# Pre-norm attention and GEGLU block on one core: permutation matmuls in the prologue, the last 512 queries in four chunks of 128, Tanh for the GELU of four chunks

## The chip, the cores and the metric

The kernel runs on one NeuronCore of a Trainium2 chip. Time is device microseconds of one execution; times of before are of three runs. The profile is of one further execution, taken by the hardware profiler.

## The reference, cut to what matters

One sequence of 2048 rows, 640 features, 32 heads of 20; a feed-forward of 1728. All inputs are bf16.

```python
def _A_ref(x, wqkv, wo):                       # H = 32, Dh = 20
    qkv = (x @ wqkv).reshape(B, S, 3, H, Dh).transpose(2, 0, 3, 1, 4)
    q, k, v = qkv[0], qkv[1], qkv[2]
    p = softmax(einsum("bhqd,bhkd->bhqk", q, k) * Dh ** -0.5)
    o = einsum("bhqk,bhkd->bhqd", p, v)
    return o.transpose(0, 2, 1, 3).reshape(B, S, D) @ wo
def _B_ref(x, w_gate, w_up, w_down):
    h = gelu_tanh(x @ w_gate) * (x @ w_up)
    return h @ w_down
h = x + _A_ref(layernorm(x), A_wqkv, A_wo)
out = h + _B_ref(layernorm(h), B_w_gate, B_w_up, B_w_down)
```

## The kernel before, in words

**A planner writes the order.** Every instruction (or small group) is an `op` with an engine, a duration guessed by `c_mm`, `c_act`, `c_dve`, a priority, what it reads and writes, and the PSUM banks it takes and gives back. `Sched.schedule` plays the program through with these durations and picks, for each engine, the ready op of the best priority; `emit` writes the resulting order as a fixed stream for each engine, with semaphore waits. So an engine is a strict queue at run time: an instruction that waits holds all behind it. `P_QK` is the best priority (scores and exponentials), `P_BG` the last (feed-forward). `QK_LEAD` and `PE_AGE` shape when TensorE leaves other work for the next scores; `WARM_*` and `PAD_*` put idle matmuls in to keep its clock up.

**Prologue.** SP loads x in four pieces of 512 rows, then the weights. For each 128 rows `ln_stats` (DVE) or `act_stats` (ScalarE, a Copy and a Square pass with accumulators; rows 512 to 1023) gives mean and variance, `ln_rsqrt` the factor through a Sqrt on ScalarE, `ln_apply` the normalised rows on DVE; five transposes on TensorE and a copy (ScalarE, or DVE for `T_DVE`) give `xnT`. `proj_k`, `proj_q`, `proj_v` project. A group is four heads, each on 32 partitions (20 used, row 0 an offset), so q and k rows must be spread from 20 to 32: `proj_k(0)` and `proj_q(0, 0)` do it by DMAs from the projected tile straight into `kt_all` and `qt_all`, the other groups by way of DRAM. `q_bound0` adds an upper bound of the scores, which needs the largest |k| of all 2048 keys. Idle rows are filled by memsets: two fills of `qt_all` on ScalarE, the others on POOL (`cst`).

**Attention.** `SIZES` cuts the queries into chunks: 512, five of 256, two of 128; a slot is a chunk and `512 / size` groups, 32 slots in all. A tile is 512 score columns of one head; 64 tiles to a slot. `unit` takes three or two tiles in turn (PSUM banks 0-2 and 3-4, `PAT`): score matmuls (L1001), one Exp on ScalarE over 1536 or 1024 columns into `pts` or `rege`, later the products with v (`pv_op`) into bank 6. `D_QUADS` gives the sets of four tiles in each slot whose exponential DVE computes instead (`d_exp`, L925 and some integer and fp16 passes over 1024, or 2048 from slot `D_WIDE` on); for slots in `DA_SLOTS` the last sum of that is an accumulating DMA issued by POOL. `D_LEAD` starts these tiles ahead of their slot. At the end of a slot `epilogue` copies bank 6, transposes it by fp32 matmuls and divides (L1098 to L1107).

**Feed-forward.** When a chunk has all its groups, `post` transposes, projects by `wo`, adds x, normalises, and issues gate matmuls (L1179) and copies (L1214), GELU on ScalarE over up to 2048 columns, up matmuls and products (L1228), then `down` (L1259, L1263). All but the last chunk do this as background while the next chunks' attention runs. Each session of GELU loads its function table and afterwards that of Exp again; `MERGE = (1,)` lets chunks 1 and 2 share one. The last chunk (`tail`) runs alone at the end, with GELU straight from PSUM (L1201, L1204).

Of the kernel before, what the change touches and what calls it, by code (L numbers as in the profile page):

```python
# [7 lines left out]
ALU = mybir.AluOpType  # L8
# [10 lines left out]
WARM_WIN, WARM_MIN = 3.4, 0.5  # L19
PAD_WIN, PAD_MIN = 3.4, 0.42  # L20
QK_LEAD = .65
PE_AGE = 1.5
SD_ALONE = .21
P_SD = 1
# [23 lines left out]
class Sched:  # L48
# [48 lines left out]
    def schedule(self):  # L97
# [23 lines left out]
        while done < total:  # L121
            assert events, "no operation can start"
# [3 lines left out]
            for e in ENGINES:  # L126
# [122 lines left out]
                for o in ([o, join] if join is not None else [o]):  # L249
                    o.start = t0 if o is chosen else free[e]  # L250
                    if e == "act":
                        due = t + o.dur + (0.905 if o.dur > 1.2 else 1.332) - QK_LEAD if o.mode == "exp" else None
# [27 lines left out]
    def emit(self, es, block_of):  # L280
# [3 lines left out]
        prog = {e: [] for e in ENGINES}  # L284
        for o in self.order:
# [8 lines left out]
            for d in o.deps:  # L294
# [78 lines left out]
D_LEAD = ((0,) * 8, (0, 10, 20) + (36,) * 21)  # L373
D_WIDE = 18
RSQRT_MAGIC = float(0x5F3759DF)

P_EV = 1.8
P_QK, P_PV, P_PRO, P_EPI, P_LN, P_BG = 0, 1, 1.5, 2, 2.5, 3
P_LND, P_LNP = 1.9, 2.5


def bass_sequential_preLN__mha_block__glu_gated_geglu__prompt_kernel(
# [12 lines left out]
    with ExitStack() as es:  # L395
# [13 lines left out]
        def c_act(n):  # L409
            return 0.052 + n * 0.000833  # L410
# [8 lines left out]
        off0 = sb("off0", [128, 1], FP32)  # L419
        stats = sb("stats", [128, 4, 2, 6], FP32)  # L420
# [3 lines left out]
        asum = sb("asum", [128, 2, 4], FP32)  # L424
# [34 lines left out]
        carve = carver(regw, W_WORDS)  # L459
        xnT = carve(NA * S).rearrange("p (a s) -> p a s", a=NA)  # L460
        wqk = carve(NA * 1280).rearrange("p (a d) -> p a d", a=NA)
        wv = carve(NA * D).rearrange("p (a d) -> p a d", a=NA)
        k_un = [carve(S), rege[:, 0:S]]
# [10 lines left out]
        xn_p = carve(4 * D).rearrange("p (i d) -> p i d", i=4)  # L474
# [50 lines left out]
        def cst(fn, key, n=128):  # L525
            op(POOL, fn, 0.1 + n * 0.001, P_BG, writes=[key, "pool"])
# [5 lines left out]
        op("act", I("activation", f32(qt_all[:, 1, :, :]), zer[:, 0:2].bitcast(FP32).to_broadcast([128, 2048]), ACT.Copy), 1.8, P_QK,  # L532
           reads=["zer"], writes=["qf1"])
        op("act", I("activation", f32(qt_all[:, 2, :, :]), zer[:, 0:2].bitcast(FP32).to_broadcast([128, 2048]), ACT.Copy), 1.8, P_QK,
           reads=["zer"], writes=["qf2"])
        op("act", I("activation", v_all[:, :, :, DH], zer[:, 0:1].unsqueeze(2).to_broadcast([128, NT, H]), ACT.Copy, bias=1.0), 0.5, P_QK,
           reads=["zer"], writes=["vones"])
        op("dve", I("memset", f32(kt_all[:, 1:4, :]), ones2), 4.2, P_QK, writes=["kf0"])
        cst(I("memset", kt_all[:, 0, :].bitcast(FP32), ones2), "ktm0", 1024)
# [3 lines left out]
        for g in range(4, NG):  # L543
            cst(I("memset", kt_all[:, g, :].bitcast(FP32), ones2), "kf%d" % g, 800)
        cst(I("memset", qt_all[:, 0, 0, :].bitcast(FP32), 0.0), "qtm0", 256)
# [7 lines left out]
        cst(I("memset", sel0, 0.0), "sel0")  # L553
        cst(I("memset", off0[:], 0.0), "off0", 1)
        for j in range(4):
            cst(I("memset", off0[32 * j:32 * j + 1, :], OFF), "off0", 1)
        cst(I("memset", identf[:], 0.0), "identf")
        cst(I("affine_select", out=identf[:], in_=identf[:], compare_op=ALU.not_equal, fill=1.0,
              base=0, pattern=[[-1, 128]], channel_multiplier=1), "identf")
        for g in range(0, NG, 2):  # L560
            cst(I("memset", f32(qt_all[:, 3, g:g + 2, :]), 0.0), "qf3%d" % g, 512)
# [4 lines left out]
        def load(dst, src, key, mb, after=(), writes=None):  # L566
            return op("sp", I("dma_start", dst, src), 0.08, P_BG, writes=writes or [key], after=after,
                      sem=key, lat=mb)
# [7 lines left out]
        load(wqk, A_wqkv[:, 0:1280].rearrange("(a p) d -> p a d", p=128), "wqk", 14.0)  # L576
# [4 lines left out]
        q_fills = [["qf0%d" % g for g in range(1, NG, 2)], ["qf1"], ["qf2"], ["qf3%d" % g for g in range(0, NG, 2)]]  # L581

        e_ops, sqrts = [], []
        T_DVE = (11, 13, 15)
# [11 lines left out]
        def ln_rsqrt(t0, n, prio, table=False, sqrt=False):  # L596
# [7 lines left out]
            d = v if table or sqrt else lambda fn, r, w: op(POOL, fn, 0.25, prio, reads=r, writes=w)  # L604
            d(I("tensor_copy", mv16[:, t0:t0 + n, :], mv[:, t0:t0 + n, :]), [("mv", t) for t in ts], [k16])
            d(I("tensor_scalar", sd16[:, t0:t0 + n], mv16[:, t0:t0 + n, 1], LN_EPS, None, ALU.add), [k16], [ks])
# [5 lines left out]
            if sqrt:  # L612
                sqrts.append(op("act", I("activation", sd16[:, t0:t0 + n], sd16[:, t0:t0 + n], ACT.Sqrt), 0.2, 1, reads=[ks], writes=[ks]))
                v(I("reciprocal", y, sd16[:, t0:t0 + n]), [ks], rk)
                return
            if table:
                op("act", I("activation", sd16[:, t0:t0 + n], sd16[:, t0:t0 + n], ACT.Sqrt), 0.2, -1, mode="sqrt", reads=[ks],
                   writes=[ks])
                v(I("reciprocal", y, sd16[:, t0:t0 + n]), [ks], rk)
                return  # L620
# [10 lines left out]
        def ln_apply(eng, src, dst, dkey, t, rkeys, prio, first=False):  # L631
# [5 lines left out]
            return op(eng, fn, 0.82 if eng == "act" else c_dve(D, 0.46), prio,  # L637
# [18 lines left out]
        def dma_transposes(src, rkeys, dst, wkey, after=()):  # L656
            op("sp", I("dma_start_transpose", dst, src), 1.25, P_EPI, reads=rkeys, writes=[wkey], sem=f"xp{wkey[1]}", lat=2.8, after=after)
# [10 lines left out]
        def act_stats(t0, n):  # L668
            for t in range(t0, t0 + n):
                for f, k in ((ACT.Copy, 0), (ACT.Square, 1)):  # L670
                    op("act", I("activation", junk, x_sb[:, t, :], f, accum_out=asum[:, k, t - t0:t - t0 + 1]), 0.86, 1.4,
                       reads=[f"x{t // 4}"], writes=["junk", ("as", t)])
            m = mv[:, t0:t0 + n, 0]
            rk = [("as", t) for t in range(t0, t0 + n)]
            d = lambda fn, r, w: op("dve", fn, 0.17, P_EPI, reads=r, writes=w)
            d(I("tensor_scalar", m, asum[:, 0, 0:n], 1.0 / D, None, ALU.mult), rk, ["am"])
            d(I("tensor_tensor", asum[:, 0, 0:n], m, m, ALU.mult), ["am"], rk)
            d(I("scalar_tensor_tensor", out=mv[:, t0:t0 + n, 1], in0=asum[:, 1, 0:n], scalar=1.0 / D, in1=asum[:, 0, 0:n],
                op0=ALU.mult, op1=ALU.subtract), rk + ["am"], [("mv", t) for t in range(t0, t0 + n)])

        for t0 in (0, 4, 8, 12):
            if t0 == 4:
                act_stats(4, 4)
            else:
                for t in range(t0, t0 + 4):
                    ln_stats(x_sb[:, t, :], t, [f"x{t // 4}"], 1.4 if t0 == 12 else P_BG)
            ln_rsqrt(t0, 4, P_PRO, sqrt=True)
            for t in range(t0, t0 + 4):
                e_ops.append(ln_apply("dve", x_sb[:, t, :], xn_p[:, t % 4, :], ("xnp", t % 4), t, [f"x{t // 4}"], P_PRO,
                                      first=True))  # L690
                transposes(xn_p[:, t % 4, :], [("xnp", t % 4)], xnT[:, :, t * 128:(t + 1) * 128], ("xnT", t),
# [3 lines left out]

        w_readers = []
# [25 lines left out]
        def proj_qk(col, t, c, dst, dkey, banks, prio, evac, after=(), peak=None):  # L722
            bk = Bank(*banks)
            key = ("bk", sc_id())
            w_readers.extend(chain(bk, key, 512, [(wqk[:, a, col + 128 * t:col + 128 * t + 128],
                                                   xnT[:, a, c * 512:(c + 1) * 512]) for a in range(NA)],
                                   [("xnT", tt) for tt in range(4 * c, 4 * c + 4)] + ["wqk"], prio))
# [18 lines left out]
        def proj_k(t, banks, prio, evac="dve"):  # L746
            for c in range(4):
                src = k_un[t % 2][:, 512 * c:512 * c + 512]
                proj_qk(D, t, c, src, ("ku", t % 2, c), banks, prio, evac, after=e_ops if t == 1 else (), peak=True)
                if t == 0:  # L750
# [24 lines left out]
        def proj_q(t, c, banks, prio, evac="dve"):  # L775
            proj_qk(0, t, c, q_un[:, t, :], ("qu", t), banks, prio, evac)
            if t == 0 and c == 0:
                for j in range(4):
                    q_keys[0][0].append(("q", 0, 0, j))
                    dma(qt_all[32 * j + 1:32 * j + 21, 0, 0, :], q_un[DH * j:DH * j + DH, 0, :], ("q", 0, 0, j),  # L780
                        [("qu", 0), "qtm0"], "qc", 2.2, prio - 0.1)
# [26 lines left out]
        def q_bound0(banks, prio):  # L808
            bk = Bank(*banks)
            key = ("bk", sc_id())  # L810
            w_readers.append(op("pe", lambda eng: eng.matmul(
                bank(bk), sel0.rearrange("p j e -> p (j e)"), aq[0], start=True, stop=True),
                c_mm(512), prio, mode="full", util=0.213, reads=[("aq", 0), "sel0"], writes=[key], acq=[bk]))
            dst = qt_all[:, 0, 0, :]
            q_first.append(op("dve", lambda eng: eng.scalar_tensor_tensor(
                out=dst, in0=bank(bk), scalar=off0[:, 0:1], in1=dst, op0=ALU.add, op1=ALU.add), c_dve(512) + 0.05, prio,
                reads=[key, "off0"] + q_keys[0][0], writes=[("qo", 0, 0)], rel=[bk]))
# [20 lines left out]
        for c, (q0, nq) in enumerate(CHUNKS):  # L838
# [516 lines left out]
```

## Time and profile before

| | |
|---|---|
| median of the runs | 910.08 us (909.8 to 910.76) |
| profiled execution | span 906.4 us; the profile gives no time around it |
| first exponential starts, last one ends | 32.86 us, 875.99 us |
| exponentials on ScalarE | 358 of 1536 columns, 349 of 1024 |
| tiles on DVE | 276 of 2048 |
| activation table loads | 16 |
| granted TensorE clock | 1.000 |

Times of the profile count from the span's start. A group's mean is the time of one instruction by itself; neighbours on an engine overlap a little, so the distance between two starts is shorter than the mean.

### The profile page before, as it was taken

To read this page: it belongs to the slowest core of one execution; us is meant where nothing else is said; L and a number is where in the kernel's file an instruction comes from. 1 tells how busy PE (TensorE), PEld (TensorE's weight loads), DVE (VectorE), ACT (ScalarE), POOL (GpSimd) and SP (SyncE) were. 2 spreads that over 40 slices of the span, in tenths; PEclk is the share of its full clock that TensorE was granted. 3 is DMA by queue.
4 is the path that set the end of the run, shared out by engine and by line. 5 is a ranking of instruction groups with operands and counts; after the bars stand their busy time and mean duration, and the time that the engine had idled before them with its cause. 6 is when DMAs were issued, how large, how long until landed. Compare 5 with 4: busy or idle time off the path is not lost.

```text
span 906.4 us, 25256 instructions
## 1 busy us (share of the span) xinstructions
PE 832.6 (92%) x11167; PEld 376.8 (42%) x11167; DVE 740.7 (82%) x1405; ACT 877.0 (97%) x793; POOL 123.5 (14%) x238
## 2 busy tenths in 40 slices
PE   3999999999898988999999999999999998998998
PEld 2432322222233332334344445444444444656666
DVE  8858898989899997898898877787977996778643
ACT  7899999999999999999999999999999999999992
POOL 5001110000013111111222000030101000101000
PEclk9999999999999999999999999999999999999999
DMA  7213341442634322243263221441432332242110
GB/s 261 84 32 80 69 97 31 106 105 62 198 136 77 56 52 48 48 69 73 49 115 63 48 44 29 84 85 41 93 63 43 75 69 39 58 85 56 33 41 16
DMA packets 52357, 65.97 MB, mean 73 GB/s; under 512 B 20876, under 2 KB 38376, under 8 KB 52248
## 3 DMA queue, kind: packets, MB, share of 16 engines
q0 software_dynamic: 12816, 31.46, 19.4%
q1 hardware_dynamic: 39432, 32.89, 13.2%
q8 instruction: 88, 1.44, 0.7%
q14 instruction: 21, 0.17, 0.1%
HBM read 20.12 MB, written 8.09 MB: 31 GB/s over the span
## 4 chain that ended last, share of the span: by engine, by line
ACT 82%; PE 13%; DVE 4%; POOL 1%; issue 0%
ACT pts L403 52%; ACT rege L403 28%; PE ps L702 4%; PE ps L1001 3%; PE ps L1179 2%; PE ps L403 2%; ACT L403 1%; PE ps L1259 1%; DVE dwx L403 1%; DVE qt_all L925 0%; PE ps L644 0%; DVE rege L1228 0%; ACT qt_all L403 0%; POOL nw L403 0%; DVE rege L925 0%
## 5 line engine op out<-in xcount | busy, mean ns | idle before, releaser
L403 ACT ACTIVATE pts<-ps 128x1536 bf16<-128x1536 f32 (+1 forms) x474 | 565.3, 1373 | 3.9 <-PE ps L403 2.9
L1001 PE MATMUL ps<-qt_all,kt_all 32*128 32x256 bf16 (+2 forms) x4096 | 308.9, 272 | 39.1 <-ACT pts L403 18.1
L403 ACT ACTIVATE rege<-ps 128x1536 bf16<-128x1536 f32 (+1 forms) x233 | 292.7, 1379 | 0.5 <-PE ps L403 0.4
L1001 PEld LDWEIGHTS ps<-qt_all,kt_all 32*128 32x128 bf16 x4096 | 102.4, 92 | 252.8 <-ACT pts L403 128.6
L1179 PE MATMUL ps<-rege,regw 128*128 128x256 bf16 (+2 forms) x1120 | 159.2, 274 | 10.2 <-ACT rege L403 2.7
L403 PE MATMUL ps<-pts,v_all 128*21 128x256 bf16 (+2 forms) x2370 | 124.8, 274 | 0.0
L1179 PEld LDWEIGHTS ps<-rege,regw 128*128 128x128 bf16 x1120 | 86.1, 98 | 62.5 <-issue 27.6
L925 DVE TENSOR_SCALAR rege<-ps 128x512 int16<-128x512 f32 x120 | 81.9, 686 | 22.2 <-PE ps L1001 21.1
L925 DVE TENSOR_SCALAR qt_all<-ps 128x512 int16<-128x512 f32 x104 | 71.2, 686 | 27.1 <-PE ps L1001 26.4
L403 PE MATMUL ps<-rege,v_all 128*21 128x256 bf16 (+2 forms) x1366 | 91.1, 278 | 0.1
L702 PE MATMUL ps<-regw 128*128 128x512 bf16 (+1 forms) x360 | 87.5, 353 | 1.9 <-ACT regw L650 1.5
L1259 PE MATMUL ps<-regw,rege 128*128 128x320 bf16 x448 | 83.8, 302 | 2.5 <-DVE qt_all L925 0.7
L403 DVE TENSOR_TENSOR qt_all<-qt_all 128x1024 int16<-128x1024 f16 (+3 forms) x77 | 68.7, 893 | 1.1
L403 PEld LDWEIGHTS ps<-pts,v_all 128*21 128x21 bf16 x2370 | 54.8, 91 | 32.7 <-issue 27.8
L403 DVE TENSOR_SCALAR qt_all<-qt_all 128x1024 int16<-128x1024 int16 (+3 forms) x106 | 57.9, 549 | 1.6 <-DMA qt_all<-dwx 0.4
L403 DVE TENSOR_TENSOR rege<-rege 128x1024 f16<-128x1024 f16 (+1 forms) x74 | 50.4, 681 | 0.7
L1259 PEld LDWEIGHTS ps<-regw,rege 128*128 128x128 bf16 x448 | 36.4, 98 | 35.0 <-issue 16.6
L403 PE MATMUL ps<-kt_all,zer 128*32 128x512 bf16 x568 | 48.3, 385 | 0.0
L403 DVE TENSOR_SCALAR rege<-rege 128x1024 int16<-128x1024 int16 (+2 forms) x113 | 47.8, 437 | 0.4
L702 PEld LDWEIGHTS ps<-regw 128*128 128x128 bf16 x360 | 28.9, 99 | 44.1 <-issue 24.4
L1214 DVE CAST rege<-ps 128x512 bf16<-128x512 f32 (+1 forms) x53 | 35.9, 678 | 13.3 <-PE ps L1179 13.1
L1228 DVE TENSOR_TENSOR rege<-rege,ps 128x512 bf16<-128x512 bf16 (+1 forms) x53 | 35.7, 676 | 12.2 <-PE ps L1179 12.1
(114 smaller groups left out, 766.2 us busy)
## 6 DMA issues: line engine op xcount, KB each, us to landing
qt_all<-qt_all POOLq DMA_DIRECT2D x9, 512.0 KB, 5.0
qt_all<-dwx POOLq DMA_DIRECT2D x9, 512.0 KB, 4.6
rege<-rege POOLq DMA_DIRECT2D x16, 256.0 KB, 3.5
rege<-dwx POOLq DMA_DIRECT2D x7, 512.0 KB, 4.8
rege<-in_A_x_dram SPq DMA_DIRECT2D x5, 640.0 KB, 5.7
dvx<-qt_all POOLq DMA_DIRECT2D x6, 512.0 KB, 4.8
q_rows<-regw SPq DMA_DIRECT2D x20, 128.0 KB, 2.8
out_dram<-rege SPq DMA_DIRECT2D x16, 160.0 KB, 3.2
```

Source lines behind the costliest of these rows:

```text
L403: return lambda eng: getattr(eng, method)(*args, **kwargs)
L702: yield op("pe", lambda eng, l=l, r=r, k=k: eng.matmul(bank(bk, n), l, r, start=(k == 0), stop=(k == len(steps) - 1)), c_mm(n) + cold, pri ...
L925: d_ops.append(op("dve", lambda eng: eng.tensor_scalar(v[:, 512 * h:512 * h + 512], bank(b), EXP_MUL, -32000.0, ALU.mult, ALU.max), c_dve( ...
L1001: return lambda eng: eng.matmul(out()[:, kk * nq:(kk + 1) * nq], kt_all[32 * j:32 * j + 32, g, kt * 128:(kt + 1) * 128], qt_all[32 * j:32 ...
L1179: op("pe", lambda eng, a=a, f=f, fi=fi: eng.matmul(bank(bk)[:, fi * nq:(fi + 1) * nq], w[:, a, F0[f]:F0[f] + 128], hnT[:, a, 128 * tb:128 ...
L1214: cp.append(op("dve", lambda eng, bg=bg, fv=fv, w=w: eng.tensor_copy(fv, bank(bg, w)), c_dve(w), p, reads=[kg], writes=hkeys(k), rel=[bg], ...
L1228: hdone.append(op("dve", lambda eng, bu=bu, fv=fv, w=w: eng.tensor_tensor(fv, fv, bank(bu, w), ALU.mult), c_dve(w), p, reads=[ku] + hkeys( ...
L1259: op("pe", lambda eng, f=f, o=o, hf=hf, bk=bk: eng.matmul(bank(bk, 320), ha_f[:, o:o + 128], wd[:, f, hf * 320:(hf + 1) * 320], start=(f = ...
```

## The change

It changes several parts at once.

- **Prologue.** A constant `perm` spreads 20 rows to 32 by a matmul: the keys 1536 to 2047 of group 0, and group 0's queries inside `q_bound0`. `wqk` is loaded as `wk` and `wq`; the projections of these keys run in pieces of 128 rows. Statistics on ScalarE go to the last one, one, three, one tiles of each four (`LN1_ACT`), seven of sixteen `ln_apply` to POOL (`LN1_POOL`), small norm steps to POOL, and the fills of `qt_all` and most of `kt_all` to POOL behind the norm.
- **Slots.** The first 512 queries run as one chunk for groups 0 to 5 and as two of 256 for groups 6 and 7; the last 512 in four chunks of 128 (`SIZES`, `QR`). The very last slot is cut into three groups and one. `FOUR`: two slots take two tiles by two. 33 slots. `SIX` (six banks in four slots) goes.
- **DVE's tiles.** 280 instead of 276; fewer slots in `DA_SLOTS`.
- **GELU.** Chunks 4, 6, 7, 8 (`TANH`) form it with Tanh on ScalarE over 512 columns and fp16 steps on DVE, in rounds of 4 (or 2) blocks; the others stay with GELU, chunks 0 and 1 and 2 and 3 in one session each.
- **Tail.** The last chunk's transposes are cut in two, its copies go to DVE, and it has priority `P_END`.
- **Loads and planner.** `w_gate` is loaded from slot 4 on, the feed-forward weights in pieces each behind the one before; constants of the planner change.

```diff
-WARM_WIN, WARM_MIN = 3.4, 0.5
-PAD_WIN, PAD_MIN = 3.4, 0.42
-QK_LEAD = .65
-PE_AGE = 1.5
+WARM_WIN, WARM_MIN = 3.4, 0.53
+PAD_WIN, PAD_MIN = 3.4, 0.46
+QK_LEAD = 0.55
+PE_AGE = 0.5
...
-SIZES = (512, 256, 256, 256, 256, 256, 128, 128)
-BASE = (0, 0, 2, 0, 2, 0, 2, 3)
-SIX = tuple(range(8, 12))
+SIZES = (256,) * 6 + (128,) * 4
+BASE = (0, 2) * 3 + ((0, 2, 3) if len(SIZES) == 9 else (0, 1, 2, 3))
+SIX = ()
+FOUR = (28, 29)
+PERM_C = 3
+FIRST = 6
+QR = ((0, 512),) + CHUNKS
...
-D_LAG = 8
-MERGE = (1,)
+D_LAG = 4
+MERGE = (0, 2)
+TANH = (4, 6, 7, 8)
...
-DA_SLOTS = (1, 2, 3, 5) + tuple(range(9, 32))
+DA_SLOTS = (1, 10, 11, 12, 14, 15, 16, 17, 18, 19, 20, 22, 23, 24, 27, 28, 31)
-D_QUADS = (1,) + (2,) * 11 + (3, 2) * 3 + (2, 2, 3) * 3 + (2,) * 5
+D_QUADS = (0, 2, 2, 2, 2, 2, 2, 1, 2, 2, 2, 2, 3, 2, 3, 2, 3, 2, 3, 2, 3, 2, 3, 2, 3, 2, 3, 2, 3, 2, 2, 2, 0)
+T_DVE = (0, 1, 3, 5, 9, 11, 12, 13, 14)
+LN1_ACT = (1, 1, 3, 1)
+LN1_POOL = (0, 1, 3, 5, 6, 13, 14)
...
-            return 0.052 + n * 0.000833
+            return 0.063 + n * 0.000833
...
-        op("act", I("activation", f32(qt_all[:, 1, :, :]), zer[:, 0:2].bitcast(FP32).to_broadcast([128, 2048]), ACT.Copy), 1.8, P_QK,
-           reads=["zer"], writes=["qf1"])
...
+        for k in range(1, 4):
+            for g in range(0, NG, 2):
+                cst(I("memset", f32(qt_all[:, k, g:g + 2, :]), 0.0), "qf%d%d" % (k, g), 512, e_ops)
...
+        def pieces(dst, src, key, after, m=1):
+            for k in range(0, dst.shape[1], m):
+                n = min(m, dst.shape[1] - k)
+                after = (load(dst[:, k:k + n, :], src[:, k:k + n, :], (key, k), W_LAT, after=after),) + tuple(after)[:0]
...
-                e_ops.append(ln_apply("dve", x_sb[:, t, :], xn_p[:, t % 4, :], ("xnp", t % 4), t, [f"x{t // 4}"], P_PRO,
+                e_ops.append(ln_apply(POOL if t in LN1_POOL else "dve", x_sb[:, t, :], xn_p[:, t % 8, :], ("xnp", t % 8), t, [f"x{t // 4}"], P_PRO,
...
+                if t == 0 and c >= PERM_C:
+                    w_readers.append(op("pe", lambda eng, bp=bp, src=src: eng.matmul(bank(bp), perm[:], src, start=True, stop=True), c_mm(512), prio,
+                                        mode="full", util=0.213, reads=[("ku", 0, c), "perm"], writes=[kp], acq=[bp]))
...
         def q_bound0(banks, prio):
+            w_readers.append(op("pe", lambda eng: eng.matmul(bank(bk), perm[:], q_un[:, 0, :], start=True, stop=False),
+                                c_mm(512), prio, mode="full", util=0.213, reads=[("qu", 0), "perm"], writes=[key], acq=[bk]))
...
-            slots += [(c, tuple(range(g, g + n))) for g in range(0, NG, n)]
+            slots += [(c, tuple(range(g, g + n))) for g in (range(FIRST) if c == 0 else range(FIRST if q0 < 512 else 0, NG, n))]
+        slots[-1:] = [(slots[-1][0], slots[-1][1][:-1]), (slots[-1][0], slots[-1][1][-1:])]
...
-        PAT = [((0, 1, 2), (3, 4, 5)) if s_ in SIX else ((0, 1, 2), (3, 4)) for s_ in range(len(slots))]
+        PAT = [((0, 1, 2), (3, 4, 5)) if s_ in SIX else ((0, 1), (2, 3)) if s_ in FOUR else ((0, 1, 2), (3, 4)) for s_ in range(len(slots))]
...
+            elif c in TANH:
+                for k0 in range(0, nb, nt_):
+                    for k in range(k0, min(k0 + nt_, nb)):
+                        bg, kg = mms(k, wg, "wg", tuple(x for key in hkeys(k) for x in sc.rd.get(key, ())))
+                        op("dve", lambda eng, bg=bg, fv=fv, w=w: eng.tensor_scalar(fv, bank(bg, w), 0.5, None, ALU.mult), c_dve(w), p, reads=[kg],
+                           writes=hkeys(k), rel=[bg], after=first)
+                        d(I("tensor_tensor", z, f2, f2, ALU.mult), 0.53, hkeys(k), [tk], aft)
+                        d(I("tensor_scalar", z, z, 8 * 0.044715 * GELU_C, 2 * GELU_C, ALU.mult, ALU.add), 0.265, [tk], [tk])
+                        d(I("tensor_tensor", z, z, f2, ALU.mult), 0.53, hkeys(k) + [tk], [tk])
+                        tanhs.append(op("act", I("activation", z, z, ACT.Tanh), c_act(w) + 0.04, P_TANH, mode="exp", reads=[tk], writes=[tk]))
+                    for k in range(k0, min(k0 + nt_, nb)):
+                        bu, ku = mms(k, wu, "wu", (sc.lw[tk],))
+                        op("dve", lambda eng, bu=bu, z=z, w=w: eng.scalar_tensor_tensor(
+                            out=z, in0=z.bitcast(F16), scalar=1.0, in1=wide(bank(bu, w)), op0=ALU.add, op1=ALU.mult), c_dve(w), p,
+                           reads=[ku, tk], writes=[tk], rel=[bu])
+                        hdone.append(op("dve", I("tensor_tensor", wide(fv), wide(fv), z, ALU.mult), 0.066 + 0.53 * w / 1024, p,
+                                        reads=[tk] + hkeys(k), writes=hkeys(k)))
...
+                if g == W_EARLY:
+                    pieces(wg, B_w_gate.rearrange("(a p) f -> p a f", p=128), "wg", tuple(w_readers))
```

More of the change, by code (lines that the diff above doesn't have):

```diff
@@ L121, in schedule @@
         while done < total:
+            if not events and due is not None and due > t:
+                events.append(due)
             assert events, "no operation can start"
@@ L293, in emit @@
             need = {}
-            for d in o.deps:
+            deps = set(o.deps)
+            if o.eng == "pool" and o.sem is None:
+                deps.update(pool)
+                pool = [o.i]
+            for d in deps:
                 q = ops[d]
@@ L616, in ln_rsqrt @@
             if table:
[L617 removed]
+                op("act", root, 0.2, -1, mode="sqrt", reads=[k16, "eps"],
                    writes=[ks])
@@ L673, in act_stats @@
             m = mv[:, t0:t0 + n, 0]
+            s0, s1 = asum[:, 0, t0:t0 + n], asum[:, 1, t0:t0 + n]
             rk = [("as", t) for t in range(t0, t0 + n)]
[L675 to L679, printed above, removed]
```

338 lines of the change are left out of this document (208 added, 130 removed).

## Prediction, before the changed kernel was run

> **What bounds the kernel now.** I read the page first (shares of the engines, chain that ended last), then ScalarE's groups kept apart by shape, its timeline, the windows, and the chain in order of time at both ends. The page:
>
> ```profile
> PE 832.6 (92%) x11167; PEld 376.8 (42%) x11167; DVE 740.7 (82%) x1405; ACT 877.0 (97%) x793; POOL 123.5 (14%) x238
> ...
> ACT 82%; PE 13%; DVE 4%; POOL 1%; issue 0%
> ```
>
> ScalarE (ACT) is busy 97% of the span and holds 82% of the chain. Its groups by shape say with what:
>
> ```profile
> L403 ACT ACTIVATE pts<-ps 128x1536 bf16<-128x1536 f32 x238 | 373.3, 1583 | 3.9 <-PE ps L403 2.9 <-PE ps L1001 0.8
> L403 ACT ACTIVATE pts<-ps 128x1024 bf16<-128x1024 f32 x236 | 270.4, 1161 | 0.0
> L403 ACT ACT_TABLE_LOAD x16 | 20.5, 1283 | 1.1 <-PEq L1340 0.8
> ```
>
> Exponentials over 1536 and 1024 score columns alternate, with no idle time before them; 16 table loads cost 1.28 us each. The means overlap, so the price of one is the distance of starts, from the timeline of ACT:
>
> ```profile
> 510.03 4.64 ACT L403 ACTIVATE pts<-ps 128x1536 bf16<-128x1536 f32 x4
> 514.49 2.43 ACT L403 ACTIVATE rege<-ps 128x1536 bf16<-128x1536 f32 x2
> ...
> 539.54 1.28 ACT L403 ACT_TABLE_LOAD   x1
> 540.83 6.46 ACT L403 ACTIVATE rege<-rege 128x2048 bf16<-128x2048 bf16 x4
> 547.31 1.28 ACT L403 ACT_TABLE_LOAD   x1
> ```
>
> The four at 510.03 are two pairs of 1536 + 1024 and take 4.46 us, 2.23 a pair; the two means differ by 0.42. So 1.33 us and 0.905 us. A GELU session is two loads round 3.24 us for each 2048 + 1536 columns (6.48 for two). Windows, in two answers (busy PE, PEld, DVE, ACT, POOL):
>
> ```profile
> 33.00:876.00 843.00, 788.84 (x10700) 345.86 (x10699) 701.10 (x1295) 838.46 (x731) 110.63 (x202) 1.00 0.33 70
> 250.00:300.00 50.00, 43.67 (x649) 16.93 (x646) 47.40 (x103) 49.80 (x43) 12.56 (x33) 1.00 0.38 96
> ```
>
> From the first exponential (32.86) to the end of the last (875.99) ACT hardly rests. And where VectorE (DVE) is 95% busy, 250 to 300, ACT still is at 49.80 of 50: a loaded DVE has not held it up so far. The ends, from the chain in order of time:
>
> ```profile
> 15.86 1.20 ACT regw L650 x2
> ...
> 17.12 4.75 PE ps L702 x14
> ...
> 32.86 4.62 ACT pts L403 x4
> ...
> 874.65 1.34 ACT rege L403
> ...
> 878.82 1.71 ACT rege L403
> ...
> 886.72 3.28 PE ps L1259 x23
> ...
> 891.07 8.01 PE ps L1179 x140
> ```
>
> The prologue waits for ACT until 17.1 and then for PE; after the last exponential come 30.4 us in which a GELU, a projection, a norm and a whole feed-forward of 128 rows go one after the other.
>
> So time = first exponential + ACT's work and stalls to the last one + tail. Before: 32.9 + 843.1 + 30.4 = 906.4, the profiled span. The profile gives no time around the span; the median of the runs is 910.08, so I carry 3.7 us over.
>
> **The middle.** Counted in the built order: before 358 x 1.33 + 349 x 0.905 = 792.0; seven GELU pairs (columns of chunks 0 to 5) x 3.24 = 22.7; ten loads x 1.30 = 13.0. Sum 827.7, so 15.4 of the 843.1 are stalls, mostly pieces of 0.03 to 0.6 us after a 1024.
> After: 332 x 1.33 + 386 x 0.905 = 790.9 (four tiles more go to DVE, but two slots run with 1024 alone); five GELU pairs 16.2, for chunks 4, 6, 7, 8 leave GELU; six loads, since MERGE pairs 0 with 1 and 2 with 3 and only chunk 5 is alone: 7.8; and 19 Tanh of 8960 columns: x 0.000833 = 7.5, and 0.13 for each (3.24 less 3584 x 0.000833, halved) = 2.4, so 9.9. Sum 824.8, 2.9 less. This includes the last chunk but one, whose GELU stood in the tail before.
>
> The loads are priced by their row, 1.28 us. [...]
>
> Stalls: I keep 15.4, and 2 for 19 Tanh that each wait in ACT's queue for DVE, with all exponentials behind them (nothing to 0.5 us each, the size of the stalls of now; 0.1 taken, as the four GELU at 540.83 started right behind their load). New QK_LEAD, PE_AGE and planner costs only reorder PE; they may take half of the stalls away or add as much: 8 either way. Middle: 842.2.
>
> **What covers it.** DVE pays. Added: three 16-bit passes and a last product for each 512 Tanh columns (0.33 + 0.20 + 0.33 + 0.33 us), 17.5 blocks: 21 us. Tiles whose last sum is done by a DMA fall from 240 to 168, so 76 more sums of about 0.30 us (0.61 for two): 22. Four exp tiles more, 1.5 each: 6. One product instead of two in the epilogues: -2. So 47; by distances of starts (0.61 us for a read of 512 from PSUM) the whole of DVE's program, counted line by line, grows from 696 to 744 us. From slot 20 on I count 278 us of DVE against some 300 of ACT, 93%; the same slots had 76%, and single slots of before 93 to 95% (144 to 167, 243 to 269, 635 to 659) without a stall of note. So I charge nothing, and keep the cost of that cover being gone as a rival. POOL issues fewer DMAs; PE's columns are the same: QK for a unit takes 0.33 us as 3 of 512, 6 of 256 or 12 of 128. The pieces of wg, wu and wd stand in SP's queue each behind the landing of the one before; what waits behind them there are x rows and transposes for chunks from 3 on, needed tens of us later.
>
> **The prologue.** Two fills of ACT (3.6 us) move to POOL behind the norm; statistics on ACT grow from 4 tiles to 6 (0.83 a pass), but only two tiles stand ahead of the first root instead of four. DVE does three tiles of x0 to about 8.0 (before: fourth one and others to 11.6); cast on POOL 0.34, root 0.2, reciprocal 0.2: 9.3. Then POOL applies three of the four. The trace has no such POOL row: at least 0.36 (DVE's distance for it), at most 0.07 + 640 x 1.75 ns = 1.2 by the slope of the affine selects (288 ns for 128 columns, 344 for 160). I take 1.1, POOL's own kind: 12.6. Transposes and copy 0.8: first K projection at 13.4 instead of 17.1. PE's list from there to the first scores is as long as before (45 wide matmuls and 20 of 128 against 53), 15.4: first exponential at 28.8. DVE's own list, 20 us of work from 5.2 on, ends earlier, at 27 with the waits. Permutation matmuls replace eight small DMAs of 0.7 us issue; those of K are needed 48 tiles later, those of q before the sum on PE: nothing on the path. Bounds 26.5 (POOL at 0.4) to 32.5.
>
> **The tail.** From the last exponential: PV 0.5; copy of 128 columns instead of 512, one transpose instead of four, reciprocal and product, last transpose and copy, two last Wo steps: 2.9. Two additions and statistics 1.6, one down addition, aggregate and casts 0.7: 5.2; root, reciprocal, apply 0.8: 6.0. PE has 27 down matmuls in its queue ahead of the transposes, 27 x 0.142 from 2.9 on: 6.7; transposes and copy 0.9: feed-forward at 7.6 instead of 15.1 after the end. What follows is unchanged (15.3): 22.9 instead of 30.4. Gone are the switch to GELU and its 1.7, 70 feed-forward matmuls and half the down projection of the chunk before. Bounds 21 to 26.
>
> Sum: 28.8 + 842.2 + 22.9 = 893.9, and 3.7: 897.6 us.
>
> **Rivals.** (a) DVE becomes the bound: 278 us of work in the last third, in a strict order with waits for PE in it. If that order fills DVE to 85% only (the slots of before lie between 66 and 95%), the stretch takes 327 instead of 300, and PE and ACT wait behind late evacuations: 924.6, slower. It decides against the whole gain from 88% down. For it: average 76% before. Against it: the 250-to-300 window. Half of it, 90%, gives 907. (b) POOL's applies come late and the prologue gains nothing: 32.9, so 901.7. For it the rows
>
> ```profile
> L403 POOL TENSOR_SCALAR nw<-nw 128x2 f32<-128x2 f32 x14 | 5.0, 360 | 1.1
> L403 POOL TENSOR_SCALAR nw<-nw 128x1 f32<-128x1 f32 x2 | 0.4, 190 | 0.2
> ```
>
> where one more column, beside a busy DVE, costs 170 ns. [...] (c) Stalls halve under the new lead times (-8), with prologue and tail at their short ends (-2.3, -1.9): 885.4. (d) The change does not do what it says: the built order has ten loads and no load near a Tanh, so I give that nothing.
>
> **How the numbers follow.** Forecast 0.55 (its own range 892 to 904), (b) 0.12, (c) 0.13, (a) in full 0.12, half of it 0.08. A measurement of this kernel tells 0.2%, 1.8 us, from no change: 908.3 to 911.9. Faster: forecast, (b), (c) and half of half-(a): 0.83; same 0.05; slower 0.12. The range reaches from (c) past half of (a) to the last case that is not slower, and leaves out full (a): 885 to 911.
>
> **What would show it.** First exponential near 29 us; ten table loads; exponentials 332 and 386 at unchanged distances; tail near 23 us. Wrong if ACT has idle time before exponentials or Tanh released by DVE or by PE after 550 us, if DVE stands at 99% there, or if POOL's 640-column applies take well over 1.2 us.

## The result, and the profile after

The changed kernel takes 898.12 us (median of four runs, 897.33 to 898.97) against 909.98 (909.8 to 910.76) of the kernel before beside it: ratio 0.987, 95% interval 0.9856 to 0.9884. The forecast was 897.6. The profiled execution has a span of 895.8 us and took 897.33, so 1.5 us lie around the span. By the three pieces of the prediction's sum:

| us | before | predicted | after |
|---|---|---|---|
| first exponential | 32.9 | 28.8 | 32.2 |
| first to end of last exponential | 843.1 | 842.2 | 840.7 |
| last exponential to the end | 30.4 | 22.9 | 22.9 |
| median less span | 3.7 | 3.7 | 2.3 |

So the total is right to 0.5 us because a miss of 3.4 us at the front is balanced by 1.5 in the middle and 1.4 in what was carried over; that they cancel is luck. The page after, shares of the engines and the chain that ended last:

```profile
PE 838.3 (94%) x12804; PEld 421.5 (47%) x12836; DVE 778.7 (87%) x1467; ACT 866.3 (97%) x811; POOL 123.9 (14%) x254
...
ACT 48%; PE 25%; DVE 22%; POOL 2%; DMA 2%; issue 1%
```

ScalarE (ACT) is as busy as before, but its share of the chain falls from 82 to 48%, and VectorE (DVE) has 22 instead of 4. The chain now changes hands: ACT, DVE and PE are late at nearly the same time. ScalarE's groups by shape:

```profile
L426 ACT ACTIVATE pts<-ps 128x1536 bf16<-128x1536 f32 x222 | 341.5, 1538 | 3.3 <-PE ps L1065 1.6 <-PE ps L426 1.3
L426 ACT ACTIVATE pts<-ps 128x1024 bf16<-128x1024 f32 x258 | 282.2, 1107 | 1.0 <-PE ps L1065 0.8
L426 ACT ACT_TABLE_LOAD x10 | 12.8, 1283 | 0.9 <-PEq L1465 0.8
L426 ACT ACTIVATE qt_all<-qt_all 128x512 f16<-128x512 f16 x16 | 10.5, 677 | 0.0
L426 ACT ACTIVATE qt_all<-qt_all 128x256 f16<-128x256 f16 x3 | 1.4, 483 | 0.0
```

Ten loads, 332 and 386 exponentials (the rest of both shapes write `rege`), as counted, and 19 Tanh in the last two rows; starts of exponentials still lie 1.330 and 0.904 us apart. What is left of the middle when the work of ScalarE is taken off, its waits, is 16.9 us. Windows (busy PE, PEld, DVE, ACT, POOL):

```profile
350.00:400.00 50.00, 48.75 (x706) 23.13 (x703) 49.55 (x104) 50.00 (x45) 8.87 (x20) 1.00 0.21 39
600.00:650.00 50.00, 49.20 (x700) 24.97 (x698) 48.05 (x84) 50.00 (x47) 5.83 (x5) 1.00 0.33 68
700.00:750.00 50.00, 45.55 (x1141) 28.84 (x1138) 45.98 (x71) 48.63 (x42) 5.94 (x15) 1.00 0.19 33
```

With DVE at 99 and at 96% ACT rests nowhere; it waits most from 700 to 750, where DVE has less to do. From 550 to 873 us ScalarE waits 2.3 us for scores (0.3 before), and 1.2 of these come through two other engines. From the timelines of POOL, DVE, PE and ACT:

```profile
735.90 1.23 DVE L426 TENSOR_TENSOR qt_all<-qt_all 128x2048 f16<-128x2048 f16 x1
735.99 1.22 POOL L426 TENSOR_SCALAR sd<-mv 128x1 bf16<-128x1 bf16 x1
742.33 0.16 DVE L426 RECIPROCAL rs<-sd 128x1 f32<-128x1 bf16 x1 [1.94 <-POOL sd L426]
743.73 0.63 PE L1065 MATMUL ps<-qt_all,kt_all 32*128 32x128 bf16 x24 [1.43 <-DVE qt_all L989]
744.17 1.45 ACT L426 ACTIVATE pts<-ps 128x1536 bf16<-128x1536 f32 x1 [1.22 <-PE ps L1065]
```

A norm's small step on POOL takes 1.22 us instead of 0.19 beside a pass of VectorE, and the next one 1.15 beside the next pass; further small steps follow them. VectorE's queue then stands 1.94 us at the reciprocal that needs the last of these, and behind it stands the read of PSUM that TensorE waits for. So DVE's rest in this window is itself a wait.

### The profile page after: what moved, and what is told of

Read it like the earlier page. It is cut to its first block, busy times and chain, and to the rows that moved or that the text cites. A ratio compares the mean times of both kernels' runs of the same rounds, so it can differ in the third digit from the quotient of the medians.

```text
span 895.8 us, 28648 instructions
## 1 busy us (share of the span) xinstructions
PE 838.3 (94%) x12804; PEld 421.5 (47%) x12836; DVE 778.7 (87%) x1467; ACT 866.3 (97%) x811; POOL 123.9 (14%) x254
## 4 chain that ended last, share of the span: by engine, by line
ACT 48%; PE 25%; DVE 22%; POOL 2%; DMA 2%; issue 1%
ACT pts L426 31%; ACT rege L426 17%; PE ps L1065 7%; DVE qt_all L426 6%; PE ps L426 5%; PE ps L1267 4%; PE ps L737 4%; PE ps L1382 3%; DVE dwx L426 3%; DVE qt_all L989 3%; DVE stats L426 1%; DVE dvx L989 1%; DMA rege<-o_nat 1%; DVE rege L989 1%; POOL nw L426 1%
## 5 line engine op out<-in xcount | busy, mean ns | idle before, releaser
L1065 PE MATMUL ps<-qt_all,kt_all 32*128 32x256 bf16 (+2 forms) x4736 | 315.9, 257 | 25.7 <-ACT pts L426 11.9
L1065 PEld LDWEIGHTS ps<-qt_all,kt_all 32*128 32x128 bf16 x4736 | 118.8, 92 | 217.6 <-ACT pts L426 94.6
L1267 PE MATMUL ps<-rege,regw 128*128 128x256 bf16 (+1 forms) x1400 | 162.1, 253 | 6.7 <-ACT rege L426 2.2
L1267 PEld LDWEIGHTS ps<-rege,regw 128*128 128x128 bf16 x1400 | 102.3, 98 | 53.8 <-issue 25.2
L737 PE MATMUL ps<-regw 128*128 128x512 bf16 (+1 forms) x333 | 80.2, 348 | 2.9 <-issue 1.3
L989 DVE TENSOR_SCALAR rege<-ps 128x512 int16<-128x512 f32 x108 | 73.3, 684 | 10.8 <-PE ps L1065 10.2
L426 DVE TENSOR_TENSOR qt_all<-qt_all 128x1024 f16<-128x1024 f16 (+5 forms) x87 | 79.6, 915 | 1.1
L426 DVE TENSOR_SCALAR qt_all<-qt_all 128x1024 int16<-128x1024 int16 (+5 forms) x131 | 66.8, 513 | 1.3
L426 PEld LDWEIGHTS ps<-rege,v_all 128*21 128x21 bf16 x1546 | 39.5, 91 | 19.7 <-issue 12.6
L989 DVE TENSOR_SCALAR dvx<-ps 128x512 int16<-128x512 f32 x60 | 40.6, 684 | 3.5 <-PE ps L1065 3.4
```

Of the source, the lines that this page charges most:

```text
L426: return lambda eng: getattr(eng, method)(*args, **kwargs)
L737: yield op("pe", lambda eng, l=l, r=r, k=k: eng.matmul(bank(bk, n), l, r, start=(k == 0), stop=(k == len(steps) - 1)), c_mm(n) + cold, pri ...
L989: d_ops.append(op("dve", lambda eng: eng.tensor_scalar(v[:, 512 * h:512 * h + 512], bank(b), EXP_MUL, -32000.0, ALU.mult, ALU.max), c_dve( ...
L1065: return lambda eng: eng.matmul(out()[:, kk * nq:(kk + 1) * nq], kt_all[32 * j:32 * j + 32, g, kt * 128:(kt + 1) * 128], qt_all[32 * j:32 ...
L1267: op("pe", lambda eng, a=a, f=f, fi=fi: eng.matmul(bank(bk)[:, fi * nq:(fi + 1) * nq], w[:, a, F0[f]:F0[f] + 128], hnT[:, a, 128 * tb:128 ...
```

## The experiments

Times are medians; the kernel before, run beside the experiments, took 909.6 to 910.6. "After" is the changed kernel, from which each experiment starts.

**The table load ahead of the first exponential.** ScalarE's timeline of after:

```profile
29.57 0.69 ACT L801 ACTIVATE kt_all<-ps,one 128x512 bf16<-128x512 f32 x1 [0.48 <-PE ps L796]
30.15 0.76 ACT L881 ACTIVATE v_all<-ps 128x320 bf16<-128x320 f32 x2
30.93 1.28 ACT L426 ACT_TABLE_LOAD   x1
32.22 4.62 ACT L426 ACTIVATE pts<-ps 128x1536 bf16<-128x1536 f32 x4
```

The first scores start at 30.50 on TensorE, and 1.72 us pass until the exponential. Before, scores started at 32.43 and the exponential came 0.43 us later, its load (31.48 to 32.76) lying ahead of and beside the scores. In the emission:

```diff
+ if e == "act" and j == first - WARM_BACK:   # WARM_BACK = 6; first: index of the first exponential
+     self.xwarm(eng)                         # Exp of one column into nm[:, 1:2]
```

> One dummy exponential of one column is put into ScalarE's program six instructions ahead of the first real one, so the Exp table is loaded in ScalarE's gap near 26.5 us. Nothing else moves. Theory (the scores of the first tile are there at 30.9 and the first exponential waits for the 1.28 us load behind the copies): first exponential at 30.9 to 31.1 instead of 32.2, total 1.2 us less, about 896.9. Rival (PE's order or VectorE sets it; the load only fills a wait): first exponential within 0.3 us of 32.2, time 898.

Measured: 896.7 us (896.62 to 896.86), ratio 0.9847 (0.9832 to 0.9862).

```profile
26.79 1.28 ACT L430 ACT_TABLE_LOAD   x1
...
31.22 4.62 ACT L430 ACTIVATE pts<-ps 128x1536 bf16<-128x1536 f32 x4
```

The load now lies in ScalarE's gap, scores start at 30.79 and the exponential follows 0.43 us later. The theory holds: 1.3 of the 3.4 us are this load. (In the nine kernels with the unchanged prologue, after among them, the scores start between 29.75 and 30.77, see the last section; the way from there to the exponential is 1.72 to 1.74 us in each, with this one change 0.43.) What it is worth in total is less certain: the profiled span falls by 0.5 only (895.8 to 895.3), since the scores came 0.3 later and the middle is 0.5 longer; and of the 1.4 between the medians a part may be the clock, for all four runs here show a mean granted clock of 1.000 and three of after's four 0.998 (the fourth took 897.33). No kernel of the study had a lower median.

**Order of the first reciprocal.** The kernel above, and the reciprocal moved ahead of two statistics:

```diff
+ for j in dv[17:15:-1]:                 # dv: DVE's places in the order
+     self.order.insert(dv[18], self.order.pop(j))
```

> The early table load of the earlier run, and VectorE's first reciprocal is put ahead of two of the three statistics that it stood behind, so POOL's first apply can start near 9.9 us instead of 10.6. Theory (the late start of the first K projection is passed on to the first scores, since TensorE's list from there is dense): first exponential 0.5 to 0.9 us earlier than with the early load alone, time 895.8 to 896.3. Rival (later chunks' statistics hold the chain, the start does not count): first exponential unchanged, time 896.7.

Measured: 896.83 us, ratio 0.9848 (0.9827 to 0.9868); first exponential at 31.24. The reciprocal starts at 9.46 instead of 10.11, and nothing follows from it. POOL's timeline of this kernel:

```profile
9.80 0.29 POOL L433 TENSOR_SCALAR_AFFINE_SELECT identf<-identf 128x128 f32<-128x128 f32 x1
10.24 0.19 POOL L433 TENSOR_TENSOR mv<-asum 128x1 f32<-128x1 f32 x1
10.54 2.83 POOL L433 TENSOR_SCALAR rege<-rege,mu,rs 128x640 bf16<-128x640 bf16 x3
```

The applies stand in POOL's queue behind the identity and a piece of the next chunk's statistics, and start at 10.54 instead of 10.55. So the first K projection did not move either (14.86, with the early load alone 14.89), and whether an earlier one would be passed on to the scores is not tested by this run; another queue holds it than the one I had moved.

**All applies on VectorE.** `LN1_POOL = ()`.

> All sixteen applies of the first norm go to VectorE (0.40 us each there, 0.87 to 1.05 us on POOL). Theory (the last 1.3 us ahead of the first exponential are the table load in ScalarE's queue, the rest PE's and VectorE's chain of copies and maxima; POOL's applies are not on it): first K projection about 1 us earlier, near 14, first exponential within 0.7 us of 32.2, time 897.5 to 899. Rival (the prediction's: POOL's applies come late): first exponential 1.5 to 2.5 us earlier, 30 to 30.7, time 895.5 to 896.5.

Measured: 898.23 us, ratio 0.9863 (0.9848 to 0.9878). First K projection at 14.52 instead of 14.94, first exponential at 33.63: later, not earlier. Moving POOL's applies away gains nothing: without them VectorE is the late one, and its copies and largest |k| end at 30.9 instead of 28.9 in the chain that ended last.

**Statistics dealt as before.** `LN1_ACT = (0, 4, 0, 0)`.

> The first norm's statistics are dealt out as in the kernel before: ScalarE takes the four tiles of chunk 1, VectorE all others. POOL's applies, Tanh and the rest stay. Theory (the new dealing brings the first K projection forward, since two tiles less stand ahead of the first root, but the copies and the table load behind it give most back): first K projection 1 to 2 us later than 14.9, first exponential 32.5 to 33.5, time 898.5 to 900. Rival (the dealing of the statistics is where the prologue lost what was predicted): first exponential at 29 to 31, time 895 to 897.

Measured: 901.46 us, ratio 0.9897 (0.9879 to 0.9915). First K projection at 17.24 (before: 17.12), first exponential at 34.34. So the dealing brings the projection 2.3 us forward and the first exponential 2.1, and 3.3 us of the total, somewhat more than expected; the rest lies in the middle, 2.4 us longer in this profile, which has a dip of the clock at 748 to 752 that after's lacks (last section).

**Chunk 8 back on the GELU table.**

```diff
- TANH = (4, 6, 7, 8)
+ TANH = (4, 6, 7)
- P_LATE = 2.4
+ P_LATE = 3
```

> Chunk 8 alone goes back to the GELU table and to the priority of the other chunks, so its GELU, up and down products stand behind the last exponential as in the kernel before; chunks 4, 6, 7 keep Tanh and everything up to 800 us is as in the changed kernel. Theory (the 7.4 us of the tail are chunk 8's work, which Tanh lets in between the exponentials): first exponential unchanged, last exponential 2 to 3 us earlier than in the changed kernel (four Tanh fewer, 2.0, and a little less for VectorE), tail 30 to 31, time 903 to 904. Rival (the tail is short because of its own priorities, P_END and the early first part of the last transposes): tail 23 to 25, time 896 to 898.

Measured: 899.87 us, ratio 0.988 (0.9865 to 0.9896). The tail is 27.0, the middle 1.1 us shorter than after's, although it holds a dip of the clock near 746. Neither theory: 4.0 of the 7.5 us of the tail go with chunk 8's Tanh and its priority `P_LATE`, which change together here, and 1.1 of these are paid ahead of it; between the medians 1.75 are left. The chain in order of time, first after, then this kernel:

```profile
877.18 0.88 DVE stats L426 x2
...
879.99 0.47 PE ps L674 x5
...
881.02 7.99 PE ps L1267 x140
889.01 3.82 PE ps L1382 x28
```

```profile
875.39 0.89 DVE stats L426 x2
...
876.92 1.30 PE ps L1267 x20
...
879.80 3.85 PE ps L1382 x28
883.65 7.82 PE ps L1267 x140
```

The last feed-forward (140 matmuls) starts 8.1 us after the last exponential in after, 12.3 here; between stand the last up matmuls of chunk 8 and its whole down projection (3.85). In the kernel before it was 15.1.

**The tail's priority.** `P_END = 2` instead of 0.5.

> The instructions behind the last exponential get the priority of the kernel before (2 instead of 0.5); chunk 8 keeps Tanh, the last transposes stay in two parts. In the built order only some six matmuls of the down projection and one addition change places. With chunk 8 on GELU the tail had been 27.0 us, with everything as before 30.4, so 3.4 us belong to something else. Theory (they belong to this priority together with the copy of 128 columns): tail 24 to 26, time 899.5 to 901. Rival (the priority is worth only the matmuls that change places, 0.14 us each, and the 3.4 us lie in the split transposes and the switch of tables): tail 22.9 to 23.7, time 898 to 899.

Measured: 899.66 us, ratio 0.989 (0.9862 to 0.9919); tail 23.8. The rest of that profile's gap to after lies in the middle, where this execution has a stretch at half clock near 745 us (last section). So the priority gives about 0.9, and, if the parts add up, some 2.6 us of the tail (7.5 - 4.0 - 0.9) stay with what I did not take apart: the transposes in two parts and the moved table loads.

**No Tanh, and Tanh for chunk 8 alone.** `TANH = ()`, then `TANH = (8,)`, both with `MERGE = (0, 2, 4, 6)`.

> The changed kernel with no chunk on Tanh: all GELU by ScalarE's GELU table, chunks in pairs 0+1, 2+3, 4+5, 6+7, and chunk 8 alone behind the last exponential. Theory (the tail's gain is the work of chunk 8 that Tanh lets run between exponentials, and Tanh is nearly neutral in the middle): tail back to about 30 us from 22.7; middle 840.9 + 2.6 (two loads more) + 6.5 (GELU of chunks 4, 6, 7) - 9.9 (Tanh) = 840; time about 905. Rival one (the tail is short because of the priorities and the 128-row chunk): tail stays at 23 to 24, time 898. Rival two (VectorE's Tanh passes cost hidden time in the middle): middle 832 to 836, time about 899 in spite of a 30 us tail.

> Only chunk 8 keeps Tanh; chunks 4+5 and 6+7 are paired on the GELU table. Theory (Tanh pays in the tail alone; elsewhere it swaps two loads and 6.5 us of GELU for 7.9 us of Tanh): tail 22 to 23, two loads more, middle 841 to 842, time 897.5 to 899.5, the same as the changed kernel. Rival (VectorE at 92 to 96% in the last third costs time): VectorE has some 17 us less to do, ScalarE's stalls from 700 to 800 us go from 4.4 to under 2, middle 836 to 839, time 893 to 896.

Measured: 913.64 us (ratio 1.0034, 1.0021 to 1.0047) and 913.02 (1.0036, 1.002 to 1.0051). All theories are far off: the whole gain is gone in both. The tail of the first is 23.8, since the planner put chunk 8's GELU between the exponentials; its middle is 857.8. (In the profiled execution of the second the granted clock of TensorE was 0.50 for some 30 us, from 784 to 814, so sums of its stages are not compared.) ScalarE's timeline of the kernel without Tanh, and TensorE's:

```profile
815.75 1.95 ACT L426 ACTIVATE pts<-ps 128x1024 bf16<-128x1024 f32 x2
828.03 3.28 ACT L426 ACTIVATE pts<-ps 128x1024 bf16<-128x1024 f32 x3 [10.33 <-PE ps L1065]
```

```profile
821.92 4.80 PE L1267 MATMUL ps<-rege,regw 128*128 128x128 bf16 x83
```

One wait of 10.3 us: the scores stand in TensorE's strict queue behind 28 down matmuls, 83 gate and up matmuls in one piece and the projection by `wo`. Ten table loads instead of six in the middle are 5.1 us; the waits behind exponentials sum to 29.9 us instead of 16.9. So 10.3 of the 17.1 us that the middle is longer are one place in the order that the planner wrote for the changed pairs, and the trace of the second kernel has the same wait, 10.33 us, at 838. The two runs therefore give no price of Tanh itself; how much is Tanh and how much the new order they do not separate.

**More and less work for VectorE, order unchanged.** An instruction whose result nobody uses, at every 12th (24th) operation of VectorE in a stretch, behind that operation's waits and ahead of its own work:

```diff
  for k, c in waits:
      eng.wait_ge(sems[k], c)
+ if e == "dve" and o.start > 550 and j % 12 == 0:
+     self.xextra(eng)                   # tensor_reduce of 256 columns of zeros
  for fn in o.fns:
```

> From 550 us on a dummy reduction over 256 columns is put into VectorE's program behind every twelfth instruction, 48 of them, about 0.35 us each by half the distance of the 512-column ones, some 17 us in all; no result is used. VectorE goes from 297 to some 314 of the 323 us between 550 us and the last exponential (97%). Theory (a loaded VectorE costs little until its work alone exceeds the time): middle 0 to 3 us longer, time 898 to 901. Rival (the one that the prediction priced: waits in VectorE's strict order leave it bound well under 100%): the 17 us show up nearly in full, time 908 to 915, with ScalarE idle before exponentials.

> The 256-column dummy reduction behind every twenty-fourth instruction of VectorE from 550 us on, 22 of them, 7.5 to 9 us in all. The run with 44 lengthened the middle by 12.8 us; taking 10 us away changed nothing. Theory (a kink at the present load, from which every piece counts): middle 5 to 7 us longer, time 903 to 905. Rival (a threshold above the present load: the first 8 us are still hidden): 0 to 2 us longer, time 898 to 900.

> The same dummy reductions behind every twelfth instruction, but from 50 to 373 us, where VectorE is busy 282 of 323 us (87%) instead of 297 (92%); some 46 of them, 16 to 19 us. Theory one (VectorE's total work decides): there are 41 us free, so 0 to 4 us longer, time 898 to 902. Theory two (the strict order decides: an instruction that the plan does not hold delays the next evacuation wherever it stands, even with free time later): 9 to 13 us longer, time 907 to 911.

And less: the three 16-bit passes ahead of each Tanh on a sixteenth to a thirty-second of the columns (`z[:, :, 0:8]`), so that this kernel leaves out most of the polynomial.

> The three 16-bit passes of VectorE ahead of each Tanh work on 16 of the 512 columns (8 of each 256, or 8 of each 128); the order of all instructions stays, the polynomial is left undone for the other columns. VectorE has about 0.55 us x 17.5 = 10 us less to do from 550 us on. The run with 44 reductions more (15 to 18 us) had lengthened the middle by 12.8 us. Theory one (there is a kink: up to the changed kernel's load VectorE is hidden, beyond it most of the work shows): middle shorter by 0 to 2 us, by the stalls at 700 to 800 us alone; time 896 to 898. Theory two (VectorE's order sets the pace from 550 us on already, at 92% busy): 5 to 8 us shorter, time 890 to 893.

| | DVE added, us | middle, us | time, us | ratio, 95% |
|---|---|---|---|---|
| less, from 550 | -9 | 841.2 | 896.9 | 0.9851 (0.9834-0.9867) |
| after | 0 | 840.7 | 898.12 | 0.987 (0.9856-0.9884) |
| 22 more, from 550 | +9.0 | 847.2 | 904.4 | 0.9932 (0.9912-0.9953) |
| 44 more, from 550 | +17.9 | 853.5 | 910.24 | 0.9996 (0.9983-1.0009) |
| 48 more, 50 to 373 | +19.8 | 851.3 | 908.8 | 0.9987 (0.9973-1.0) |

The row of the added reductions (busy, mean), with 44:

```profile
L428 DVE TENSOR_REDUCE scr<-zer 128x1 f32<-128x256 bf16 x44 | 17.9, 407 | 1.3 <-PE ps L1172 0.7 <-PE ps L1271 0.4
```

Each costs the middle 0.30 (22), 0.29 (44) and 0.22 us (48; the profile with 44 has two dips of the granted clock, the other two have none). Less work gives nothing in the middle of the profile (which has a dip of the clock at 744 to 748 that after's lacks) and 1.2 us between the medians; more work counts from the first piece: a kink at the present load. And it depends little on how full VectorE is: from 50 to 373 us it was busy 282 of 323 us, 87%, and 10.7 us are lost all the same; from 550 on 297 of 323, 92%. Each added piece stands behind a wait, so a rest just ahead of it cannot take it up; pieces put ahead of the waits were not tried and could cost less. The chain that ended last, with 48 reductions more and with 9 us less:

```profile
DVE 43%; PE 31%; ACT 21%; POOL 2%; issue 1%; DMA 1%; DVEq 0%
```

```profile
ACT 56%; PE 25%; DVE 14%; POOL 2%; DMA 2%; issue 1%
```

It moves to VectorE and back to ScalarE, through a kernel in which both are late together. Of the theories, the one of the strict order fits (9 to 13 us expected at 87%, 10.7 measured): an instruction that the order was not made for delays what stands behind it, the reads of PSUM among it, and free time further on does not give all of that back.

## Why the prediction was right, and where not

**The middle** was right to 1.5 us in 842. By terms, measured: exponentials 790.5 (predicted 790.9); GELU 16.5 (16.2); six loads 7.7 (7.8); Tanh 9.2 (9.9; 0.52 us for 512 columns instead of 0.56); waits 16.9 (17.4). The halving of waits (rival c) did not happen. The 2 us taken for the waits of the 19 Tanh were not needed (no idle time ahead of them in their two rows); the other waits grew by 1.5 instead.

**What covers it** came out as counted: 92% of VectorE from 550 us on for 93% predicted. One sign of being wrong, idle time before exponentials released by PE after 550 us, did come, with 2.3 us. And the reason given (a loaded VectorE has not held ScalarE up) is only half of it. Rival (a) took a fill below which the queue cannot keep up; the runs show no such fill. Work that the order holds is covered at 96 to 99%; work that it does not hold costs over half of its busy time at 87% and nearly three quarters at 92%. The rival was nearer than its 0.20 said: 9 us more, put in without a new order, cost 6.5.

**The tail** is right in size: the last feed-forward starts 8.1 us after the last exponential for 7.6 predicted, and 14.8 us follow for 15.3. In its working, what chunk 8 leaves behind is worth 4.0 and not nearly the whole; the priority gives 0.9; the remaining 2.6 were not taken apart.

**The prologue is the step that failed**: 28.8 became 32.2, the outcome (though not the cause) of rival (b). Its terms: POOL's first apply at 9.3 was 10.6. The items named for the 9.3 (8.0 + 0.34 + 0.2 + 0.2) make only 8.7; and both queues were taken as free, while POOL's holds constants and statistics ahead of the apply and VectorE's holds three statistics ahead of the reciprocal, both until 10.42. The three applies took 2.99 instead of 3.3, which leaves 1.0 late. Transposes and copy 1.35 instead of 0.8: first K projection at 14.94 for 13.4. "PE's list as long as before, 15.4" was 16.0 from there to the point where the exponential could have started, 30.93, and it was not PE's list alone. The chain that ended last:

```profile
24.21 0.47 PE ps L674 x5
24.70 0.49 DVE regw L683
25.19 1.18 DVE kd L773 x2
...
28.35 0.53 DVE dwx L426
...
28.93 0.39 PE ps L864
```

From 24.70 to 28.88 VectorE's copy, the largest |k| of the four pieces (L773) and the bound hold the scores, where the kernel before had TensorE alone in the chain from 17.12 to 32.84; the prediction had VectorE's list off the path, ending at 27. At 30.93 a table load, which the kernel before hid ahead of and beside its scores, stood on the path: 1.3. The terms are 1.0, 0.55, 0.6 and 1.3, of which the 0.6 is within the spread that goes with the first matmuls (last section). Rival (b)'s cause, slow applies, is refuted: they were faster than taken, and with none on POOL the first exponential came later. The 170 ns that it reads from two rows are no price of a column either: in before's trace the steps of two columns between 680 and 682 us take 0.19, and one takes 1.17 (at 603.93) beside a pass of VectorE over 2048 columns (603.83 to 605.06).

**The carry-over**, 3.7, held some 2.0 around the span (1.7 to 2.2 in the runs of the kernel before beside the experiments; 1.5 to 1.6 for the changed kernels) and some 1.7 by which the profiled execution of before was under its median; the second part does not carry to another kernel. Of the chances, those named for faster add up to 0.84, not 0.83, which changes nothing.

**Not tried by itself**: the permutation matmuls, the new slots (`SIZES`, `FOUR`), the shared sessions (`MERGE`), and the planner's constants `QK_LEAD`, `PE_AGE`, `WARM_*`. What they cost or bring is only argued.

## What to carry to other kernels

Price an added instruction on a second engine by its place in the written order, not by that engine's idle share: with an order fitted to the load, ScalarE and VectorE were late together, and 0.41 us of VectorE put in by hand, behind a wait, cost 0.2 to 0.3 us even where it rested 13% of the time. An order written ahead can also lose more at one place than a change was to bring: 10.3 us at one wait in the kernel without Tanh. When a stage in front gets shorter, look at what used to lie beside it: here a table load of 1.28 us came onto the path, and one dummy exponential in an idle gap took it off again. A sum that comes out right is no proof of its terms; put each beside its own row.

## What the runs showed of the hardware

**The granted clock after a short rest.** Three of the four runs of after show a mean clock of 0.998. Windows of the kernel with the old tail priority:

```profile
740.00:744.00 4.00, 2.54 (x68) 1.57 (x52) 2.21 (x5) 2.76 (x4) 1.43 (x5) 1.00 0.73 136
744.00:746.00 2.00, 1.72 (x44) 0.93 (x44) 2.00 (x4) 1.98 (x2) 0.00 (x0) 0.79 0.38 71
746.00:748.00 2.00, 2.00 (x45) 1.16 (x34) 2.00 (x4) 1.99 (x2) 0.00 (x0) 0.50 0.03 8
748.00:750.00 2.00, 2.00 (x35) 1.90 (x35) 2.00 (x3) 1.98 (x3) 0.15 (x1) 0.86 0.00 0
```

TensorE rests for 1.46 us ahead of a set of scores, and from about 745 on runs at half clock for some 3.4 us; the profiled run of after has the same rest (1.43 us) and stays at 1.00. Of eleven profiles with this rest (1.43 to 1.60 us; all but the two without Tanh in chunks 4, 6 and 7), five show a dip that begins some 2 us behind it, six show none. So a rest of this length is not enough by itself, and what decides stays open.

**The first matmuls.** The first TensorE work of these profiles is at half the later rate, and when that ends differs from profile to profile. The column of the granted clock reads 1.00 there (windows from 14 to 20 us), so this is read from the distances of matmuls alone. TensorE's timeline of after, and of the kernel with less work for VectorE, whose prologue is the same:

```profile
18.76 1.92 PE L737 MATMUL ps<-regw 128*128 128x512 bf16 x6
```

```profile
18.13 1.59 PE L737 MATMUL ps<-regw 128*128 128x512 bf16 x7
```

Single matmuls of 512 columns start 0.427 us apart and then 0.216; the change came at 19.4 us in after, at 17.5 in the other, at 20.1 in the one with the early load. The first scores follow it: 30.50, 29.75 and 30.79. So a first exponential of one profile is good to about half a microsecond either way, and the spread is no property of the kernel. What moves the change, by 2.6 us between the earliest and the latest of these three, was not shown.

**POOL beside VectorE.** In after VectorE's apply of 640 columns starts at 10.57, ahead of POOL's at 10.60, and takes 0.40 us; POOL's takes 1.04, against 0.87 for each of the two behind it. With the reciprocal moved VectorE's starts behind POOL's, at 10.67, takes 0.92 and ends at 11.59; POOL's takes 0.88 and is over at 11.42. And a step of one column on POOL took 1.22 and 1.15 us where it started just behind a pass of VectorE over 2048 columns (1.23 and 1.18 us), and ended 0.04 to 0.08 us behind that pass; of the other twelve steps of this norm ten take 0.18 or 0.19, two 0.53 and 0.48. So each was slower where it started behind the other: VectorE's apply 0.92 us for 0.40, POOL's 1.04 for 0.87. The small steps lasted until the pass was over; of the two applies the second ends 0.17 us (VectorE's) and 0.67 us (POOL's) behind the first, less than it takes by itself, so it was not held to the end of the first. What holds the second was not shown.
